# Two transfers into an unread place in HBM, behind the halves of the next wq, at the change of layers of a decode kernel

## The chip, the cores and the metric

The kernel runs on one core of one Trainium2 chip. The metric is device time in microseconds (us): the median of 3 runs is 673.28 us (673.07 to 673.45).

## The reference

One token goes through attention over a cache, then an MLP, and both once more with the same weights and the same cache. All numbers are float32. Cut to what matters:

```
D, H, Sk, Dh, F = 512, 32, 4096, 128, 1376          # x is [1, 1, 512]

def A(x):                                            # attention over the cache
    q = (x @ wq).reshape(1, 1, H, Dh).transpose(0, 2, 1, 3)
    scores = einsum("bhqd,bhkd->bhqk", q, k_cache) * Dh ** -0.5
    o = einsum("bhqk,bhkd->bhqd", softmax(scores), v_cache)
    return o.transpose(0, 2, 1, 3).reshape(1, 1, H * Dh) @ wo

def B(x):                                            # MLP, gelu by its tanh form
    return gelu(x @ w1 + b1) @ w2 + b2

x = x + A(layernorm(x)); x = x + B(layernorm(x))
x = x + A(layernorm(x)); x = x + B(layernorm(x))
```

## The kernel before

The 32 heads are worked in 8 groups of 4. Each group has 8 MB of K and 8 MB of V (64 KB a partition each) and 1 MB each of wq and wo. One array in SBUF, `arena`, holds everything that is loaded, and the code gives each load its columns in it by hand. Every load goes through the helper `load` (line 87): one DMA issue on SyncE's queue (SP), pinned to the order in which the code writes it. So all transfers run through one hardware queue in that order; a load whose place in `arena` is still being read waits on SP, and with it everything behind it.

Each issue also takes the next of eight completion counters in turn (DMAHW0 to DMAHW7 in the rows below). It waits until the transfer that had its counter before, eight issues earlier, has landed.

Layer 0 takes the groups upwards, layer 1 downwards, so group 7 is last in layer 0 and first in layer 1. Its K and V, and part of the V of group 6, stay in SBUF over the change of layers. Between the two stands the MLP of layer 0 (`mlp`, called with `fill`): `hidden` multiplies by w1 in three parts, `gelu` follows, and a loop over 11 blocks c multiplies by w2 (line 413). w2 lies where the first loads of the next layer go. So the loop itself issues these loads, by the table `follow`: behind block 3 the rest of w2 and the tail of the first chunk of K of group 6; behind block 5 the first half of the next wq (512 KB); behind block 7 its second half; behind block 9 the first 512 KB of that chunk of K. The next wq is group 6's, for the second group of layer 1. Behind the MLP come the rest of that chunk (256 KB), a second chunk of K in two pieces of 512 KB, then two of 1 MB, one of 4 MB, and so on.

With the MLP done, layer 1 makes its queries for group 7 (line 199) and multiplies with the K that stayed (line 232). Meanwhile VectorE makes the queries of group 6 from the two halves of wq (lines 213 and 215, one step for each of four blocks of rows).

`idle` (line 437) is a matmul whose result nobody reads. Only loads and one write at the end use the DMA queue.

Of the kernel before, what the change touches and what calls it, by code (L numbers as in the profile page):

```python
# [12 lines left out]
F32 = mybir.dt.float32  # L13
# [4 lines left out]
P = 128  # L18
# [9 lines left out]
U = 512  # L28
# [25 lines left out]
LAST_IDLE = {3: 1, 5: 1, 6: 1}  # L54
WHOLE, HALVES = ((0, 8),), ((0, 4), (4, 8))
VAR_AT = 1
PAIRS = (0, 2, 4, 6), ((4, 6, 0, 2), (2, 0, 4, 6))


@with_exitstack  # L60
def decode_layers(ctx: ExitStack, tc: tile.TileContext, k, v, w, w1, w2, out):
    nc = tc.nc
# [3 lines left out]

    def ctile(name, *shape):
        return const.tile([P, *shape], F32, name=name)

    smalls, places, uses = ctile("smalls", SMALLS), {}, {}  # L70

    def small(name, n=1):

        if name not in places:
            first = sum(n * len(turns) for n, turns in places.values())
            places[name] = n, [first + n * i for i in range(2 if name in ("xs", "x_sum", "rstd", "sc", "nsc") else 1)]
        uses[name] = uses.get(name, -1) + 1
        turns = places[name][1]
        at = turns[uses[name] % len(turns)]
        assert at + n <= SMALLS and n == places[name][0]  # L80
        return smalls[:, at : at + n]
# [3 lines left out]
    def load(at, src):  # L85
        t = arena[:, at : at + src.shape[-1]]
        tc.keep_in_program_order(nc.sync.dma_start(t, src))  # L87
        return t

    def pin(ins):  # L90
        tc.keep_in_program_order(ins)
# [40 lines left out]
    wq_first = chunk(ahead[:, AHEAD:])  # L132

    ident = ctile("ident", P)
    make_identity(nc, ident)
    nc.vector.memset(negmean, -1.0 / D)
# [20 lines left out]
    def of_32(t, n, i=0):  # L157
        return t[:, : 32 * n].rearrange("p (c q) -> p c q", q=32)[:, :, i]
# [22 lines left out]
    def mean_of(xs, s, at, whole=False, xc=None):  # L181
        nm = minus_mean(s, at, whole)
        sq, ss = small("sq", 4), small("ss")
        xc = small("xc", 4) if xc is None else xc
        nc.vector.tensor_scalar(xc, xs[:, :, 0], nm, None, op0=ALU.add)
        nc.vector.scalar_tensor_tensor(sq, xc, 1.0, xc, op0=ALU.mult, op1=ALU.mult, accum_out=ss)
        return nm, ss, xc

    def rstd_of(ss, at, whole=False):
        nv = minus_mean(ss, at, whole)  # L190
        ve, r = small("ve"), small("rstd")
        tc.keep_in_program_order(
            nc.vector.tensor_scalar(ve, nv, -1.0, EPS, op0=ALU.mult, op1=ALU.add))
        nc.gpsimd.tensor_tensor(r, ve, power, op=ALU.pow)
        return r
# [139 lines left out]
    def mlp(xs, s, w1_t, w2_t, xb, rows, fill, follow):  # L335
        hs, rstd = pH[layer], []
        if fill is None:
            nm, ss, _ = mean_of(xs, s, pN[:, 0:1], True)
            nm_s, nmr, cb, late = small("nm_s"), small("negm"), colsum, HIDDEN[0][1]
            nc.vector.tensor_copy(nm_s, nm)  # L340
        else:
            centred = small("xs", 8).rearrange("p (c i) -> p c i", i=2)
            nc.gpsimd.memset(centred[:, :, 1], 1.0)
            _, ss, _ = mean_of(xs, s, pN[:, 0:1], True, centred[:, :, 0])
        nc.gpsimd.tensor_tensor(xb, xs[:, :, 0], b2c, op=ALU.add)
        if fill is not None:
            xs = centred

        def hidden(i):
            at, first = hs[i], W1_AT[i]  # L350
            n = min(32 * HIDDEN[i][1], FJ) - 32 * HIDDEN[i][0]
            for c in range(4):
                for j in range(J):
                    f = first + n * (J * c + j)
                    pin(nc.tensor.matmul(at[32 * j : 32 * j + 2, :n], xs[:, c, :], w1_t[:, f : f + n],
                                         start=(c == 0), stop=(c == 3)))
                if i == 0 and c == VAR_AT:
                    rstd.append(rstd_of(ss, pN[:, 1:2], True))
                if i == 0 and c == VAR_AT and fill is None:
                    nc.gpsimd.tensor_tensor(nmr, nm_s, rstd[0], op=ALU.mult)  # L360
                    nc.gpsimd.tensor_scalar(cb[:, late:], colsum[:, late:], nmr, None, op0=ALU.mult)
                    nc.gpsimd.tensor_tensor(cb[:, late:], cb[:, late:], b1c[:, late:], op=ALU.add)

        def turned(i):
            ht = work.tile([P, 32 * 4], F32, name="pt")
            n = HIDDEN[i][1] - HIDDEN[i][0]
            pin(nc.vector.transpose(ht[:, : 32 * n], hs[i][:, : 32 * n]))  # L367
            return ht

        def gelu(i, ht):  # L370
            b0, b1_ = HIDDEN[i]
            n = b1_ - b0
            h, u, g = (small("gelu_" + k, FB)[:, b0:b1_] for k in "hug")
            if fill is not None:
                pin(nc.vector.scalar_tensor_tensor(u, of_32(ht, n), rstd[0], b1c[:, b0:b1_], op0=ALU.mult, op1=ALU.add))  # L375
                nc.gpsimd.tensor_copy(colsum[:, b0:b1_], of_32(ht, n, 1))
            elif i > 0:
                pin(nc.vector.scalar_tensor_tensor(u, of_32(ht, n), rstd[0], cb[:, b0:b1_], op0=ALU.mult, op1=ALU.add))
            else:
                pin(nc.vector.scalar_tensor_tensor(h, of_32(ht, n, 1), nm_s, of_32(ht, n), op0=ALU.mult, op1=ALU.add))  # L380
                pin(nc.vector.scalar_tensor_tensor(u, h, rstd[0], b1c[:, b0:b1_], op0=ALU.mult, op1=ALU.add))
            nc.scalar.activation(g, u, AF.Gelu_apprx_tanh)  # L382
            if fill is not None and b1_ == FB:
                nc.scalar.activation(small("m"), g[:, :1], AF.Exp, scale=0.0)
            return g

        if fill is not None:
            idle(fill, pS, 2 * P)
        hidden(0)
        if fill is None:  # L390
            hidden(1)
            pin(nc.vector.transpose(rows[:, P : 2 * P], rows[:, :P]))
        ht = turned(0)
        if fill is None:
            hidden(2)
        else:
            idle(fill, pO)
        for i, (b0, b1_) in enumerate(HIDDEN):
            if i == 1 and fill is not None:
                for n in (512, 256):  # L400
                    idle(fill, pS, n)
                hidden(1)
                ht = turned(1)
                idle(fill, pS, 2 * P)
            g = gelu(i, ht)
            if fill is None and b1_ < FB:
                ht = turned(i + 1)
            for c in range(b0, b1_):
                if c == b0 + 2 and i == 1 and fill is not None:
                    hidden(2)  # L410
                    ht = turned(2)
                for j in range(J):
                    pin(nc.tensor.matmul(pM[32 * j : 32 * j + 1, :], g[:, c - b0 : c - b0 + 1],
                                         w2_t[c][:, P * j : P * (j + 1)], start=(c == 0), stop=(c == FB - 1)))
                for at, src in follow.get(c, ()):
                    load(at, src)
            if i == 1 and fill is not None:
                idle(fill, pS, 2 * P)

# [16 lines left out]
    def idle(t, at, n=512):  # L436
        pin(nc.tensor.matmul(at[:C, :n], ident[:, :C], t[:, 0, :n], start=True, stop=True))  # L437

    for layer in range(2):
# [23 lines left out]
        for n, g in enumerate(order):  # L463
            first, final = n == 0, n == G - 1
            pairs = None
            if layer == 0 and n < G - 2:
                pairs = PAIRS[0]
            if layer == 1 and 1 < n < G - 2:
                pairs = PAIRS[1][n % 2]

# [146 lines left out]
        if layer == 0:  # L617
# [6 lines left out]
                9: ((SPARE, first_k[:, : 2 * U]),),  # L624
            }
        mlp(x1, s1, w1_t, w2_t[layer], xb, *((None, last_v) if layer == 0 else (ends, None)), follow)
        if layer == 0:
            idle(last_v, pS, 2 * P)
# [57 lines left out]
```

## Time and profile before

| what | value |
|---|---|
| median of 3 runs | 673.28 us |
| the profiled execution | 673.77 us |
| its span | 672.0 us |
| DMA queue busy, of 16 engines | 99.1% |
| moved | 285 MB, mean 425 GB/s |
| TensorE / VectorE / ScalarE busy | 45% / 61% / 32% |
| share of the chain that ended last: DMA / TensorE / VectorE | 65% / 16% / 15% |

The span runs from the first instruction to the last; the profiled execution's own time is 1.77 us longer. The chain is followed back from the last instruction, at each step to what released it. KB in the rows are 1024 bytes; "us to landing" runs from the issue on SP to the landing of the transfer's last byte.

### The profile page before, as it was taken

To read this page: it belongs to the slowest core of one execution; us is meant where nothing else is said; L and a number is where in the kernel's file an instruction comes from. 1 tells how busy PE (TensorE), PEld (TensorE's weight loads), DVE (VectorE), ACT (ScalarE), POOL (GpSimd) and SP (SyncE) were. 2 spreads that over 40 slices of the span, in tenths; PEclk is the share of its full clock that TensorE was granted. 3 is DMA by queue.
4 is the path that set the end of the run, shared out by engine and by line. 5 is a ranking of instruction groups with operands and counts; after the bars stand their busy time and mean duration, and the time that the engine had idled before them with its cause. 6 is when DMAs were issued, how large, how long until landed. Compare 5 with 4: busy or idle time off the path is not lost.

```text
span 672.0 us, 6011 instructions
## 1 busy us (share of the span) xinstructions
PE 301.1 (45%) x2236; PEld 79.4 (12%) x2236; DVE 406.7 (61%) x510; ACT 215.4 (32%) x697; POOL 5.2 (1%) x26
## 2 busy tenths in 40 slices
PE   1501603416016053166698985604316026065597
PEld 1100100101001010011124311101001001011124
DVE  3059679497795876971422313289597794982513
ACT  0047064190560823801011200073290650910010
POOL 1000000000000000000000000000000000000000
PEclk9965855856758557586699998755757758566799
DMA  9999999999999999999999999999999999999997
GB/s 384 429 437 437 438 433 437 410 458 433 437 437 402 466 418 430 421 437 422 429 413 398 391 434 449 426 433 437 421 434 425 433 430 415 456 429 418 429 416 301
DMA packets 11548, 285.36 MB, mean 425 GB/s; under 512 B 1280, under 2 KB 1408, under 8 KB 3840
## 3 DMA queue, kind: packets, MB, share of 16 engines
q1 hardware_dynamic: 11520, 284.99, 99.1%
q8 instruction: 17, 0.28, 0.2%
q14 instruction: 11, 0.09, 0.0%
HBM read 284.92 MB, written 0.07 MB: 424 GB/s over the span
## 4 chain that ended last, share of the span: by engine, by line
DMA 65%; PE 16%; DVE 15%; issue 1%; another core or an unknown queue 1%; SPq 0%; ACT 0%; DVEq 0%; ACTq 0%
DMA arena<-in_v 38%; DMA arena<-in_k 19%; DMA arena<-in_w 8%; PE pS L232 7%; DVE arena L274 7%; PE pO L262 5%; DVE arena L279 3%; DVE arena L311 2%; DVE arena L287 1%; PE pO L283 1%; DVE arena L215 1%; PE pB L323 1%; SPq L87 0%; DVE arena L309 0%
## 5 line engine op out<-in xcount | busy, mean ns | idle before, releaser
L269 ACT ACTIVATE arena<-arena,pt 128x128 f32<-128x128 f32 x640 | 188.0, 387 | 49.1 <-DMA arena<-in_v 45.3
L232 PE MATMUL pS<-arena,smalls 128*8 128x512 f32 x1024 | 147.3, 728 | 78.6 <-DMA arena<-in_k 74.5
L279 DVE TENSOR_TENSOR arena<-arena 128x4096 f32<-128x4096 f32 x30 | 132.6, 4420 | 0.3
L217 PE MATMUL pS<-arena,smalls 128*128 128x512 f32 x20 | 20.7, 1140 | 203.4 <-DVE arena L215 203.4
L274 DVE TENSOR_TENSOR arena<-arena,pt 128x2048 f32<-128x2048 f32 x40 | 89.0, 2286 | 37.3 <-DMA arena<-in_v 34.6
L244 ACT ACTIVATE arena<-pS,smalls 128x512 f32<-128x512 f32 x16 | 12.4, 777 | 292.8 <-DVE smalls L243 292.8
L287 DVE STREAM_TRANSPOSE arena<-pO 128x512 f32<-128x512 f32 x16 | 11.5, 717 | 98.3 <-PE pO L262 60.9
L232 PEld LDWEIGHTS pS<-arena,smalls 128*8 128x8 f32 x1024 | 29.8, 102 | 199.1 <-issue 178.6
L262 PE MATMUL pO<-arena,pt 128*4 128x512 f32 x368 | 46.8, 653 | 10.8 <-DMA arena<-in_v 10.0
L236 DVE TENSOR_REDUCE smalls<-pS 128x1 f32<-128x512 f32 x16 | 11.0, 687 | 62.7 <-PE pS L232 62.7
L215 DVE SCALAR_TENSOR_TENSOR arena<-arena,smalls 128x512 f32<-128x512 f32 x45 | 33.8, 752 | 1.6
L311 DVE SCALAR_TENSOR_TENSOR arena<-arena,smalls 128x512 f32<-128x512 f32 x39 | 29.3, 752 | 1.4
L217 PEld LDWEIGHTS pS<-arena,smalls 128*128 128x128 f32 x20 | 5.0, 312 | 206.1 <-DVE arena L215 206.1
L315 PE MATMUL pB<-arena,smalls 128*1 128x512 f32 x26 | 14.1, 625 | 29.8 <-DVE arena L311 29.8
L246 PE MATMUL pO<-ident,arena 128*128 128x128 f32 x64 | 12.2, 320 | 25.6 <-ACT arena L244 25.2
L572 DVE TENSOR_TENSOR arena<-arena 128x2048 f32<-128x2048 f32 x10 | 22.9, 2292 | 0.3
L262 PEld LDWEIGHTS pO<-arena,pt 128*4 128x4 f32 x368 | 10.0, 92 | 44.4 <-issue 37.5
L382 ACT ACTIVATE smalls<-smalls 128x4 f32<-128x4 f32 (+1 forms) x6 | 1.2, 205 | 42.6 <-DVE smalls L375 24.7
L250 DVE STREAM_TRANSPOSE smalls<-smalls 128x32 f32<-128x32 f32 x16 | 3.4, 212 | 17.5 <-ACT arena L244 17.5
L437 PE MATMUL pS<-arena,ident 128*8 128x512 f32 (+1 forms) x30 | 12.9, 522 | 0.5 <-DVE pt L367 0.5
L244 ACT ACT_TABLE_LOAD x1 | 1.3, 1283 | 35.9 <-DVE smalls L243 35.9
L246 PEld LDWEIGHTS pO<-ident,arena 128*128 128x128 f32 x64 | 7.6, 155 | 39.5 <-ACT arena L244 34.1
(115 smaller groups left out, 186.2 us busy)
## 6 DMA issues: line engine op xcount, KB each, us to landing
arena<-in_w SPq DMA_DIRECT2D x13, 2048.0 KB, 12.5
arena<-in_k SPq DMA_DIRECT2D x5, 4096.0 KB, 22.3
arena<-in_v SPq DMA_DIRECT2D x2, 4096.0 KB, 32.8
arena<-in_w SPq DMA_DIRECT2D x6, 1024.0 KB, 30.7
arena<-in_k SPq DMA_DIRECT2D x1, 6144.0 KB, 21.0
arena<-in_v SPq DMA_DIRECT2D x2, 2048.0 KB, 37.3
arena<-in_w SPq DMA_DIRECT2D x7, 512.0 KB, 11.4
arena<-in_v SPq DMA_DIRECT2D x3, 1024.0 KB, 47.3
```

The costliest lines, as they stand in the source:

```text
L215: pin(nc.vector.scalar_tensor_tensor(t, wt[:, c, :], xc[:, c : c + 1], t, op0=ALU.mult, op1=ALU.add))
L217: pin(nc.tensor.matmul(at, one.to_broadcast([P, P]), t, start=True, stop=True))
L232: pin(nc.tensor.matmul(pS[32 * j : 32 * j + C, :], z[:, j, C - 1 - c : 2 * C - 1 - c], kt[:, j, :], start=(c == 0), stop=(c == C - 1)))
L246: nc.tensor.transpose(pT[:, b].rearrange("p j r -> p (j r)"), p[:, P * b : P * (b + 1)], ident)
L262: nc.tensor.matmul(pO[32 * j : 32 * j + 4, :], pt[:, j, c, :], by_head(vt)[:, j], start=(i == 0), stop=(i == of - 1))
L269: nc.scalar.activation(own, own, AF.Copy, scale=pt[:, j, c, b : b + 1])
L274: nc.vector.tensor_tensor(own, own, weight, op=ALU.mult)
L279: pin(nc.vector.tensor_tensor(a, a, b, op=ALU.add))
L287: nc.vector.transpose(ot[:, :512], pO)
L311: pin(nc.vector.scalar_tensor_tensor(t, wt[:, d, :], on[:, d : d + 1], t, op0=ALU.mult, op1=ALU.add))
L315: pin(nc.tensor.matmul(pB[0:1, :], one, t, start=n == 0, stop=n == G - 2))
L572: pin(nc.vector.tensor_tensor(total, total, other, op=ALU.add))
```

## The change

Two tiles of 128 rows of 2 KB are made in HBM. Behind the issue of each half of the next wq, one transfer copies 2 KB a partition (256 KB) of w1 from HBM into one of them. Nothing reads these tiles. It is issued on the same queue, SP's, and pinned to its place.

```
+IDLE_TRANSFERS = (5, 7)
...
+    spare_dram = ctx.enter_context(tc.tile_pool(name="spare_dram", bufs=1, space=bass.MemoryType.DRAM))
+    unread = [spare_dram.tile([P, U], F32, name=f"unread{i}") for i in range(2)]
+
+    def idle_transfer(i):
+        pin(nc.sync.dma_start(unread[i], w1[:, U * i : U * (i + 1)]))
...
                 for at, src in follow.get(c, ()):
                     load(at, src)
+                if fill is not None and c in IDLE_TRANSFERS:
+                    idle_transfer(IDLE_TRANSFERS.index(c))
```

On SP's queue, from the tail of K (128x512) through the pieces of K behind the change, stood before (L87 is `load`; the sizes are partitions x elements of 4 bytes; the names in brackets are what an issue waits for):

```order
L87 DMA arena<-in_k 128x512 [waits DMAHW5_49,PE_49]
L87 DMA arena<-in_w 128x1024 [waits DMAHW0_49,PE_49]
L87 DMA arena<-in_w 128x1024 [waits DMAHW7_49,DMAHW2_49,PE_49]
L87 DMA arena<-in_k 128x1024 [waits DMAHW3_49,PE_49]
L87 DMA arena<-in_k 128x512 [waits DMAHW4_49,DMAHW1_49,PE_49]
L87 DMA arena<-in_k 128x1024 [waits PE_49] x2
L87 DMA arena<-in_k 128x2048 [waits PE_49]
L87 DMA arena<-in_k 128x2048 [waits DMAHW5_49,PE_49]
L87 DMA arena<-in_k 128x8192 [waits DMAHW6_49,PE_49]
```

In the same place stands now (`load` is L94, the idle transfer L75):

```order
L94 DMA arena<-in_k 128x512 [waits DMAHW5_49,PE_49]
L94 DMA arena<-in_w 128x1024 [waits DMAHW0_49,PE_49]
L75 DMA unread_66<-in_w 128x512 [waits DMAHW7_49]
L94 DMA arena<-in_w 128x1024 [waits DMAHW2_49,PE_49]
L75 DMA unread_67<-in_w 128x512 [waits DMAHW1_49]
L94 DMA arena<-in_k 128x1024 [waits DMAHW3_49,PE_49]
L94 DMA arena<-in_k 128x512 [waits DMAHW4_49,PE_49]
L94 DMA arena<-in_k 128x1024 [waits PE_49]
L94 DMA arena<-in_k 128x1024 [waits DMAHW5_49,PE_49]
L94 DMA arena<-in_k 128x2048 [waits DMAHW6_49,PE_49]
L94 DMA arena<-in_k 128x2048 [waits DMAHW7_49,PE_49]
L94 DMA arena<-in_k 128x8192 [waits DMAHW0_49,PE_49]
```

Two issues came in, and the counters behind them moved on by one and by two: the last 128x2048 piece now waits for the counter that the first idle transfer uses (DMAHW7), and the one ahead of it for that of the first half of wq (DMAHW6).

On VectorE, in the queries of group 6 that use the next wq, stood before (L213 is the first block of rows, L215 the other three):

```order
L461 TENSOR_SCALAR smalls<-smalls 128x1
L213 TENSOR_SCALAR arena<-arena,smalls 128x512 [waits DMAHW6_49]
L215 SCALAR_TENSOR_TENSOR arena<-arena,smalls 128x512 [waits DVE_49]
L215 SCALAR_TENSOR_TENSOR arena<-arena,smalls 128x512 [waits DMAHW7_49,DVE_49]
L215 SCALAR_TENSOR_TENSOR arena<-arena,smalls 128x512 [waits DVE_49]
```

and now:

```order
L470 TENSOR_SCALAR smalls<-smalls 128x1
L220 TENSOR_SCALAR arena<-arena,smalls 128x512 [waits DMAHW6_49]
L222 SCALAR_TENSOR_TENSOR arena<-arena,smalls 128x512 [waits DVE_49]
L222 SCALAR_TENSOR_TENSOR arena<-arena,smalls 128x512 [waits DMAHW0_49,DVE_49]
L222 SCALAR_TENSOR_TENSOR arena<-arena,smalls 128x512 [waits DVE_49]
```

Nothing moved here; the second half of wq is waited for at the same step as before (the second of the three), under another counter's name.

## Rows read from the trace of the kernel before

**Rows 1.** The page: the DMA queue (packets, MB, share), and the chain by engine.

```profile
q1 hardware_dynamic: 11520, 284.99, 99.1%
DMA 65%; PE 16%; DVE 15%; issue 1%; another core or an unknown queue 1%; SPq 0%; ACT 0%; DVEq 0%; ACTq 0%
```

**Rows 2.** The chain in order of time: start us, us, what.

```profile
371.29 7.05 PE pS L232 x64
...
414.33 23.56 DMA arena<-in_v
...
656.72 11.43 DMA arena<-in_w
...
668.28 0.99 PE pO L413 x24
```

**Rows 3.** By stretches: us, busy time (count) of each engine, PEclk, DMA share, GB/s.

```profile
342.00:366.00 24.00, 20.75 (x296) 8.19 (x296) 3.81 (x16) 0.41 (x2) 1.13 (x4) 1.00 1.01 413
366.00:376.00 10.00, 8.76 (x137) 3.46 (x134) 5.05 (x19) 1.69 (x3) 0.84 (x3) 1.00 0.93 319
378.00:402.00 24.00, 21.95 (x158) 5.66 (x153) 3.93 (x15) 3.61 (x8) 0.00 (x0) 1.00 1.03 441
```

**Rows 4.** The timeline of SP's issues: start us, us of the issue itself.

```profile
360.74 0.38 SPq L87 DMA_DIRECT2D arena<-in_w  x1
361.22 0.38 SPq L87 DMA_DIRECT2D arena<-in_k  x1
364.78 0.33 SPq L87 DMA_DIRECT2D arena<-in_w  x1
367.01 0.33 SPq L87 DMA_DIRECT2D arena<-in_w  x1
368.37 0.33 SPq L87 DMA_DIRECT2D arena<-in_k  x1
373.25 0.33 SPq L87 DMA_DIRECT2D arena<-in_k  x1
409.13 0.33 SPq L87 DMA_DIRECT2D arena<-in_k  x1
```

**Rows 5.** DMA issues: KB, us to landing; those of rows 4, then 368.3 to 374.

```profile
arena<-in_w SPq DMA_DIRECT2D x1, 256.0 KB, 7.5
arena<-in_k SPq DMA_DIRECT2D x1, 256.0 KB, 7.7
arena<-in_w SPq DMA_DIRECT2D x1, 512.0 KB, 5.4
arena<-in_w SPq DMA_DIRECT2D x1, 512.0 KB, 4.4
arena<-in_k SPq DMA_DIRECT2D x1, 512.0 KB, 5.4
arena<-in_k SPq DMA_DIRECT2D x1, 1024.0 KB, 10.1
arena<-in_k SPq DMA_DIRECT2D x1, 2048.0 KB, 12.0
arena<-in_k SPq DMA_DIRECT2D x2, 1024.0 KB, 9.3
arena<-in_k SPq DMA_DIRECT2D x3, 512.0 KB, 6.2
arena<-in_k SPq DMA_DIRECT2D x1, 256.0 KB, 5.6
```

**Rows 6.** VectorE's timeline where it uses the next wq.

```profile
372.16 0.48 DVE L213 TENSOR_SCALAR arena<-arena,smalls 128x512 f32<-128x512 f32 x1
372.67 2.33 DVE L215 SCALAR_TENSOR_TENSOR arena<-arena,smalls 128x512 f32<-128x512 f32 x3
```

**Rows 7.** DMA issues into an empty queue: the kernel's first load, its last write.

```profile
arena<-in_w SPq DMA_DIRECT2D x1, 1056.0 KB, 4.8
out<-arena SPq DMA_DIRECT2D x1, 64.0 KB, 1.5
```

## The prediction

> **What bounds the kernel now.** I read the page's queue section and its chain first, then the chain in order of time, then the DMA share by stretches, and last the issues one by one. One hardware queue moves 285 MB and keeps 16 engines 99.1% busy, and 65% of the chain that ended last is DMA [rows 1]. The chain ends in a transfer that lands at 668.1 us, then 1.0 us of matmuls [rows 2]. So the kernel ends when its slowest DMA engine has moved all bytes, and the rest counts only where it lets the queue run dry.
>
> It runs dry once, at the change of layers. The queue moves 413 GB/s from 342 to 366 us and 441 GB/s from 378 to 402 us, but 319 GB/s from 366 to 376 us [rows 3]. That is 10 us x (413 - 319) / 413 = 2.3 us of lost transfer time. The reader is to see that TensorE runs at its full granted clock (1.00) in all three stretches, so its clock is no part of this.
>
> The issues say where the time is lost. A transfer's last byte lands at its issue time plus its time to landing [rows 4, 5]: the 256 KB of the k tail (issued 361.22) at 368.92, the first half of the next wq (364.78) at 370.18, the second half (367.01) at 371.41, the first piece of K (368.37) at 373.77, the last of the small pieces of K (373.25) at 383.35. At 413 GB/s a piece of 512 KB takes 1.27 us. The first half of wq comes 1.26 us behind the k tail and the second 1.23 us behind the first: up to 371.41 the last engine loses nothing. The first piece of K comes 2.36 us later, so 1.09 us are lost there. From then to 383.35 are 9.58 us for 256 + 2 x 512 + 2 x 1024 KB (3328 KB, 3.41 MB), which take 8.25 us at 413 GB/s: another 1.33 us lost. Together 2.4 us, as the stretch of 10 us gave it.
>
> Behind 378 us the queue stays ahead: a K transfer issued at 409.13 lands only at 421.1 [rows 4, 5], and the load of V that the chain names is issued at 414.33 into that backlog [rows 2]. From 371 to 414 us the chain runs on TensorE and VectorE [rows 2] with data landed long before, so a small shift of the queue does not reach it. Whatever moves the landing at 383.35 moves the end by as much, unless it is lost and won again inside the change.
>
> **The change part by part.** It adds two DMA issues on SP, one behind each half of the next wq, each moving 256 KB from HBM to HBM. It removes and reorders nothing; a later load merely has one or two more transfers between it and the one that last used its completion counter.
>
> *SP's time.* An issue takes 0.33 to 0.38 us [rows 4]. The first stands between 365.1 and 367.01, the second between 367.34 and 368.37: both in gaps in which SP waits for matmuls, 1.9 and 1.0 us long. Cost nothing. If a gap were too short, the first piece of K would be issued up to 0.4 us later.
>
> *Completion counters.* There are eight in turn, so each issue waits for the transfer eight places earlier. The 1 MB piece issued at 373.25 now waits for the first idle transfer instead of an older load, and the one before it for the first half of wq, which landed at 370.18. The idle one should land near 370.9, over 2 us before it is needed. Nothing; it would cost only if that transfer took over 3 us.
>
> *The later landing of wq.* The second half lands one idle transfer later, 371.41 + 0.68 = 372.1. VectorE starts on the first half at 372.16 and needs the second for the second of its three 0.78 us steps from 372.67, at about 373.4 [rows 6]. Hidden, with 1.3 us to spare.
>
> *The bytes themselves.* This is the term that counts. The trace has no transfer from HBM to HBM. The nearest row is a load of the same 256 KB in 2 KB rows with a full queue: issued 360.74, landed 368.24, and the next such 256 KB at 368.92, so 0.68 us [rows 4, 5]. Two cost 1.36 us where the queue is full. The lower bound is zero, where they run in time that is lost anyway. The upper bound is 1.5 us each: the 64 KB that the kernel writes to HBM land 1.5 us after issue with nothing ahead [rows 7], all of it start and finish. A load into a cold queue shows as much of its own: 4.8 us for 1056 KB that take 2.6 us at 413 GB/s, 2.2 us of start and finish [rows 7], so a write to HBM does not look slower to finish than a load. I take 0.68 us.
>
> The Trainium skill speaks against that value: its page "DMA: Bandwidth & Descriptors", section "Latency and other measured facts", gives 214 GB/s per direction as the full rate of copies between HBM tensors. By it an idle transfer would take an estimated 262,144 B / 214 GB/s = 1.22 us, 2.4 us for both; no row here shows one, and the sum does not use it.
>
> *The sum for the slowest engine.* First half of wq 370.18, idle 370.86, second half 372.13, idle 372.81, first K piece 372.81 + 1.27 = 374.08 against 373.77 before: +0.31 us. Of 1.36 us added, 1.05 fill the 1.09 us that this engine lost there. Behind it the second loss, 1.33 us, is still to come. If it comes from late issues, the times of which TensorE sets, the +0.31 vanishes in it wholly or in part; so the landing at 383.35 moves by 0 to +0.3. On the engines that ran ahead the idle transfers lie wholly in time lost. I take +0.2 us. Against the profiled execution (span 672.0, 673.77 in all) that gives 674.0; that execution was 0.49 us above the median of the runs, so against the median, 673.28, it gives **673.5 us**.
>
> **The rivals.**
>
> *The queue stays warm.* A good part of the loss may not be late issue but the start of a queue run dry: the first piece of K needs 5.4 us from issue to landing though only 371.41 + 1.27 was in its way, and 2.2 us of start and finish show at the kernel's start [rows 5, 7]. If an idle transfer in front lets the engines fetch the next one's work beneath it, the second loss goes too: +0.31 - 1.33 = -1.0 us, **672.3**. Against it: the later pieces of K are issued in step with TensorE's work on the new layer, at times no idle transfer changes. Even wholly right it gives at most 2.4 - 1.36 = 1.0 us.
>
> *A packet from HBM to HBM costs more than a load (the slower side).* It reads and writes the same memory, and the engine may hold it twice as long: 1.36 us instead of 0.68. Then the second half of wq lands at 372.8, the first K piece at 371.41 + 2 x 1.36 + 1.27 = 375.4, +1.67 us, of which the second loss takes none if it is a start-up loss: **674.95**, slower. If it takes all of its 1.33, +0.3. The point is where two transfers exceed 1.05 us of cover by the 1.35 us that can be told: 1.2 us each. At the upper bound of 1.5 us it is +1.95, **675.2**. For it: the same HBM serves both sides. Against: the queue is bound by its engines at 413 to 441 GB/s whatever the load, and the write at the end shows nothing long.
>
> The rate of 214 GB/s in "DMA: Bandwidth & Descriptors" (the Trainium skill, section "Latency and other measured facts") stands behind this rival: its 1.22 us lie just at that point.
>
> *No cover.* If the first K piece came late for want of its own data path and not because of its issue time, idle work ahead of it only adds: +1.36, **674.6**, at the edge of what can be told.
>
> *It doesn't do what it says.* If a transfer from HBM to HBM were spread over few of the 16 engines, one engine would carry 256 KB alone: 16 x 0.64 = 10 us each. Nothing in the loads, all cut by 128 rows, suggests it.
>
> **How the numbers follow.** A difference of 0.2% (1.35 us) is about what a measurement of this kernel can tell from no change. Chances: forecast (-0.3 to +0.6 us) 0.54; warm queue (-1.2 to -0.3) 0.2; costlier packets 0.16, half of it over +1.35; no cover 0.07, half of it over; few engines 0.03. Faster by over 0.2% would need all the lost time back and the idle bytes free, which only a mis-read loss allows: 0.06, out of the warm queue. Slower: 0.08 + 0.04 + 0.03 = 0.15. The same: 0.79. The range goes from the warm queue's 672.3 to the costlier packet's upper bound, 675.2; the likeliest case's own is 673.0 to 673.9.
>
> **What would show it.** Right: two rows of 256 KB into the unread place that take about 0.7 us of the queue each; the stretch 366 to 376 us up from 319 GB/s by nearly the 52 GB/s that 0.52 MB bring; the second half of wq landing near 372.1, the first piece of K near 374, the last small piece at 383.0 to 383.7, and 414.33 for the issue of V unchanged. Warm queue: the last small piece near 382.3. Costlier packets: the first piece of K past 375. Wrong altogether: the matmuls or VectorE's steps at 371 to 374 us waiting for wq, or issues of K held behind the idle transfers' completion.

## The result, and the profile after

The changed kernel takes 674.23 us (median of 22 runs, 673.96 to 674.49), the kernel before 673.09 us (22 runs beside it, 672.67 to 674.82). The ratio is 1.0013, 95% interval 1.0007 to 1.0019: +0.9 us, between +0.5 and +1.3. It is estimated from all runs, so it is not the quotient of the two medians, which differ by 1.14 us. The forecast was 673.5 us, +0.2, too little to be told from no change. The measured time lies in the range and under the 0.2% bound, but clear of zero. In a second measurement (the fifth experiment) the same kernel gave 1.0007 (0.9998 to 1.0015), +0.5 us. A second difference was not forecast: the runs of before spread over 2.2 us (standard deviation 0.54), those after over 0.5 us (0.14). Beside experiments 5 to 8 one run of before fell in a slow state (712.36 us); it is left out below.

The page of after, the lines of [rows 1], and the bytes to and from HBM:

```profile
q1 hardware_dynamic: 11808, 285.51, 99.2%
HBM read 285.44 MB, written 0.59 MB: 425 GB/s over the span
DMA 63%; PE 17%; DVE 16%; another core or an unknown queue 2%; issue 1%; SPq 0%; ACT 0%; DVEq 0%; ACTq 0%
```

There are 288 packets more (2 x 128, and 16 x 2 that write the counters), and 0.52 MB more are read and written. The change does what it says. By stretches, as in [rows 3]:

```profile
342.00:366.00 24.00, 20.57 (x298) 8.00 (x298) 4.16 (x18) 0.41 (x2) 1.27 (x6) 1.00 1.00 411
366.00:376.00 10.00, 8.95 (x134) 3.57 (x138) 4.71 (x18) 1.69 (x3) 0.70 (x2) 1.00 1.04 385
378.00:402.00 24.00, 21.70 (x158) 5.57 (x152) 4.09 (x16) 3.51 (x7) 0.00 (x0) 1.00 1.05 448
```

The stretch of the change moves 385 GB/s where it moved 319. But 52 of the 66 GB/s more are idle bytes, and 319 was a low draw: two further profiles of the kernel before (experiments 1 and 9) moved 353 and 350 there:

```profile
366.00:376.00 10.00, 8.62 (x130) 3.47 (x134) 5.02 (x19) 1.69 (x3) 0.83 (x3) 1.00 0.99 353
366.00:376.00 10.00, 8.71 (x134) 3.55 (x138) 4.92 (x19) 1.69 (x3) 0.73 (x2) 1.00 0.98 350
```

SP's issues as in [rows 4], and with them those of the idle transfers (L75):

```profile
361.89 0.38 SPq L94 DMA_DIRECT2D arena<-in_k  x1
364.43 0.33 SPq L94 DMA_DIRECT2D arena<-in_w  x1
364.81 0.60 SPq L75 DMA_DIRECT2D unread<-in_w  x1
366.67 0.34 SPq L94 DMA_DIRECT2D arena<-in_w  x1
367.07 0.50 SPq L75 DMA_DIRECT2D unread<-in_w  x1
368.04 1.00 SPq L94 DMA_DIRECT2D arena<-in_k  x1
372.94 0.33 SPq L94 DMA_DIRECT2D arena<-in_k  x1
```

and the landings of the same seven, in the same order, as in [rows 5]:

```profile
arena<-in_k SPq DMA_DIRECT2D x1, 256.0 KB, 6.7
arena<-in_w SPq DMA_DIRECT2D x1, 512.0 KB, 5.4
unread<-in_w SPq DMA_DIRECT2D x1, 256.0 KB, 5.7
arena<-in_w SPq DMA_DIRECT2D x1, 512.0 KB, 5.0
unread<-in_w SPq DMA_DIRECT2D x1, 256.0 KB, 5.3
arena<-in_k SPq DMA_DIRECT2D x1, 512.0 KB, 5.8
arena<-in_k SPq DMA_DIRECT2D x1, 1024.0 KB, 10.1
```

Added up: K tail 368.59, first half of wq 369.83, idle 370.51, second half 371.67, idle 372.37, first K piece 373.84, last 1 MB piece 383.04. The idle transfers cost 0.68 and 0.70 us, the price taken (a time to landing is given to 0.1 us, so each of these differences is good to about 0.1). From the tail to the last piece are 14.45 us; the useful bytes take 12.06 (4.98 MB at 413 GB/s), so 2.39 us go elsewhere, 1.36 of them into idle bytes and 1.03 into waiting. In the profile of before the same stretch lost 2.37 us [rows 4, 5]. By these two profiles the change would cost nothing. VectorE does not notice, as in [rows 6]:

```profile
371.85 0.48 DVE L220 TENSOR_SCALAR arena<-arena,smalls 128x512 f32<-128x512 f32 x1
372.36 2.33 DVE L222 SCALAR_TENSOR_TENSOR arena<-arena,smalls 128x512 f32<-128x512 f32 x3
```

The load of V that the chain names is issued 0.2 us earlier than in [rows 2], and the chain ends 0.2 us later:

```profile
414.13 26.00 DMA arena<-in_v
...
656.95 11.40 DMA arena<-in_w
668.35 0.14 issue
668.48 1.00 PE pO L420 x24
```

Spans are 672.4 against 672.0 us, yet the medians differ by 1.1. So the question for the experiments: where does the rest come from, and how far does one profile of before stand for its runs? Each was timed beside the kernel before on the same chip. The loss given with each is that of the last engine: the time from the K tail's landing to the last 1 MB piece's, less 12.06 us. (The expectations quote some losses read more finely; they differ from those here by up to 0.05 us.) A spread is the standard deviation of a kernel's runs.

### The profile page after: what moved, and what is told of

It is laid out like the page before. It is cut to its first block, busy times and chain, and to the rows that moved or that the text cites. A ratio compares the mean times of both kernels' runs of the same rounds, so it can differ in the third digit from the quotient of the medians.

```text
span 672.4 us, 6015 instructions
## 1 busy us (share of the span) xinstructions
PE 302.4 (45%) x2236; PEld 79.7 (12%) x2236; DVE 406.8 (61%) x510; ACT 215.4 (32%) x697; POOL 5.2 (1%) x26
## 4 chain that ended last, share of the span: by engine, by line
DMA 63%; PE 17%; DVE 16%; another core or an unknown queue 2%; issue 1%; SPq 0%; ACT 0%; DVEq 0%; ACTq 0%
DMA arena<-in_v 31%; DMA arena<-in_k 24%; DMA arena<-in_w 8%; PE pS L239 8%; DVE arena L281 7%; PE pO L269 5%; DVE arena L286 3%; DVE arena L318 2%; DVE arena L294 1%; PE pO L290 1%; DVE arena L222 1%; PE pB L330 1%; DVE arena L316 1%; PE pO L233 0%
## 5 line engine op out<-in xcount | busy, mean ns | idle before, releaser
L239 PE MATMUL pS<-arena,smalls 128*8 128x512 f32 x1024 | 145.3, 720 | 79.2 <-DMA arena<-in_k 75.0
L322 PE MATMUL pB<-arena,smalls 128*1 128x512 f32 x26 | 15.8, 693 | 29.6 <-DVE arena L318 29.6
```

The source lines that it names most:

```text
L239: pin(nc.tensor.matmul(pS[32 * j : 32 * j + C, :], z[:, j, C - 1 - c : 2 * C - 1 - c], kt[:, j, :], start=(c == 0), stop=(c == C - 1)))
L322: pin(nc.tensor.matmul(pB[0:1, :], one, t, start=n == 0, stop=n == G - 2))
```

## The experiments

**1. The kernel before, again.** No edit.

> The kernel before, unchanged, profiled and timed once more: how far one profile of it stands for its median. The changed kernel measured +0.9 us (ratio 1.0013), while the two profiles differ by 0.4 us of span. Theory A (the idle bytes cost the last engine most of their 1.36 us, and the first profile of before showed more lost time at the change than a usual run has): the same time as before within 0.2 us, a span near 671.4 instead of 672.0, and less than the 2.4 us lost between the k tail's landing and that of the last 1 MB piece of K, near 1.6 us. Theory B (the cost is not at the change but a fixed one of two more issues or of another program): again 2.4 us lost there.

Median 674.08 us against 673.73; ratio 1.0008 (0.9998 to 1.0017). So the medians of kernels that are the same can stand 0.35 us apart, with 11 runs of one. Its issues of the K tail and the last 1 MB piece, and their landings:

```profile
361.94 0.39 SPq L87 DMA_DIRECT2D arena<-in_k  x1
373.25 0.33 SPq L87 DMA_DIRECT2D arena<-in_k  x1
```

```profile
arena<-in_k SPq DMA_DIRECT2D x1, 256.0 KB, 6.9
arena<-in_k SPq DMA_DIRECT2D x1, 1024.0 KB, 9.4
```

368.84 to 382.65: 1.75 us lost, not 2.37, as theory A had it (1.6). The span, 672.0, was as long as in the first profile of before, though the last piece landed 0.70 us earlier: it lost elsewhere what it gained here.

**2. Almost no bytes.**

```
-        pin(nc.sync.dma_start(unread[i], w1[:, U * i : U * (i + 1)]))
+        pin(nc.sync.dma_start(unread[i][:, :16], w1[:, U * i : U * i + 16]))
```

> The two idle transfers move 64 B a partition instead of 2 KB: same issues, places and completions, 1/32 of the bytes. Theory A (bytes): at most 0.1 to 0.2 us over the kernel before, ratio 1.0000 to 1.0003. Theory B (fixed cost of the issues, of their completions or of a write to HBM): the same +0.9 us as the changed kernel, ratio 1.0013. Theory C (an idle transfer keeps the queue warm whatever its size): faster than before by 0.2 to 1 us.

674.35 us, ratio 1.0012 (1.0003 to 1.0021); its median stands 0.27 us above that of experiment 1, an unchanged kernel, with runs that spread by 0.9. By its time this neither shows nor excludes a fixed cost. Its loss is 2.54 us (368.87 to 383.47): 64 B a partition do not keep the queue from running dry, which ends theory C. Its quickest run, 673.08, is as quick as before's (672.97), while no run of the changed kernel has come under 673.96.

**3. Twice the bytes.**

```
-    unread = [spare_dram.tile([P, U], ...
+    unread = [spare_dram.tile([P, 2 * U], ...
-        pin(nc.sync.dma_start(unread[i], w1[:, U * i : U * (i + 1)]))
+        pin(nc.sync.dma_start(unread[i], w1[:, 2 * U * i : 2 * U * (i + 1)]))
```

> The two idle transfers move 4 KB a partition, twice the bytes of the change. At 1.27 us each they add 2.54 us to each engine's queue. Theory A (bytes, the cover already used up by the first 1.36 us): +0.9 + 1.2 = +2.1 us over before, ratio 1.0031. Theory B (fixed): +0.9 us as the changed kernel, ratio 1.0013. If much of the lost time can still be filled, something between, near +1.4.

675.71 us (6 runs), ratio 1.0032 (1.0020 to 1.0044): +2.2 us as theory A had it; theory B, a cost that is all fixed (1.0013), is out. A fixed part beside the price of the bytes is not: theory A's sum takes the +0.9 of the first measurement as given. Its issues of the K tail and the last piece, and their landings:

```profile
361.07 0.38 SPq L94 DMA_DIRECT2D arena<-in_k  x1
373.13 0.33 SPq L94 DMA_DIRECT2D arena<-in_k  x1
```

```profile
arena<-in_k SPq DMA_DIRECT2D x1, 256.0 KB, 7.7
arena<-in_k SPq DMA_DIRECT2D x1, 1024.0 KB, 11.2
```

368.77 to 384.33: 3.50 us, of which 2.54 are idle bytes and 0.96 waiting. With twice the bytes the waiting stays at 1.0 us. What idle bytes can replace was replaced by the first ones; in these profiles the rest was not filled from these places.

**4. Two transfers where the queue is full.** The call moves from `mlp` to the fourth group of layer 0.

```
-                if fill is not None and c in IDLE_TRANSFERS:
-                    idle_transfer(IDLE_TRANSFERS.index(c))
...
+                if layer == 0 and n == 3:
+                    idle_transfer(0)
+                    idle_transfer(1)
```

> Both idle transfers of 2 KB a partition stand in layer 0, behind the weights of the fourth group, where the queue is never dry, instead of at the change of layers: the full price of the bytes with no cover. Theory A: +1.36 us over before, ratio 1.0020, so the change of layers covers 1.36 - 0.9 = 0.4 to 0.5 us. If a transfer from HBM to HBM cost twice a load of its size: +2.7 us, ratio 1.0040. Theory B (fixed cost of the issues): +0.9 us.

674.84 us, ratio 1.0015 (1.0006 to 1.0024): +1.0 us. The issues of the weights and the two idle transfers, and their landings:

```profile
170.01 0.33 SPq L94 DMA_DIRECT2D arena<-in_w  x1
170.39 0.59 SPq L75 DMA_DIRECT2D unread<-in_w  x1
171.04 0.58 SPq L75 DMA_DIRECT2D unread<-in_w  x1
```

```profile
arena<-in_w SPq DMA_DIRECT2D x1, 2048.0 KB, 11.6
unread<-in_w SPq DMA_DIRECT2D x1, 256.0 KB, 11.9
unread<-in_w SPq DMA_DIRECT2D x1, 256.0 KB, 11.9
```

181.61, 182.29, 182.94: 0.68 and 0.65 us each. A transfer from HBM to HBM costs what a load of its size costs, and the rival of the dearer packet falls. The +1.36 expected lies in the interval, as does theory B's +0.9. The interval (+0.4 to +1.6) also holds what the change itself cost: by these times no cover at all is shown for the change of layers.

**5. The changed kernel, again.** No edit.

> The changed kernel, unchanged, timed and profiled once more beside the kernel before. Its first measurement gave ratio 1.0013 (+0.9 us), but the profile shows its last engine losing 2.34 us at the change (1.36 us of idle bytes among them) against 2.41, 1.70 and 2.55 us in three profiles without such bytes (the kernel before, the same again, and the one with 64 B a partition). Theory A (the idle bytes fill lost time but for 0.1 to 0.7 us): +0.1 to +0.7 us, ratio 1.0002 to 1.0010, 2.0 to 2.6 us lost again. Theory B (a cost of 0.9 us or more that the change of layers doesn't show): +0.9 to +1.1 us, ratio 1.0013 to 1.0016. Both: a spread of its runs far below that of the kernel before (standard deviation 0.14 against 0.5 to 0.7 us).

674.42 us against 673.50; ratio 1.0007 (0.9998 to 1.0015), spread 0.12 us. The K tail (issued 361.11, 7.7 us to landing) lands at 368.81, the last piece (373.17, 10.1 us) at 383.27: 2.40 us lost, 1.04 of it waiting, as in its first profile (2.39, 1.03). The interval holds theory A (1.0002 to 1.0010) and B's lower end.

**6 and 7. One transfer alone.** `IDLE_TRANSFERS = (5,)`, then `(7,)`.

> Only the idle transfer behind the first half of the next wq is left. Theory A1 (the first 0.7 us of idle bytes are covered, what comes above is not, since the kernel with 4 KB a partition cost 1.2 us more than the changed one for 1.2 us more of bytes): 0 to +0.2 us against before, ratio 1.0000 to 1.0003. Theory A2 (a byte costs the same whichever it is): half of the changed kernel's cost, +0.3 to +0.5 us. If this place has no cover of its own, since the last engine loses nothing ahead of the second half of wq: +0.7 us.

> Only the idle transfer behind the second half of the next wq is left, right ahead of the first piece of K, where the engines ran dry. Theory A1: 0 to +0.2 us, ratio 1.0000 to 1.0003, and no more than with the first one alone. Theory A2: +0.3 to +0.5 us. The warm queue: faster than before by 0.2 to 0.7 us, since the engines reach the first piece of K without a break.

673.83 and 673.77 us beside 673.50; ratios 1.0001 (0.9992 to 1.0010) and 0.9999 (0.9990 to 1.0007), spreads 0.15 and 0.13 us. The two places do not differ, though one has lost time right behind it and the other has none. Losses 1.88 and 2.00 us, 1.20 and 1.32 of it waiting. No gain from a warm queue shows, though the second's interval reaches down to -0.7 us. A1 fits; A2 (+0.3 to +0.5) is not excluded.

**8. Two transfers farther back.** `IDLE_TRANSFERS = (9, 10)`.

> Both idle transfers of 2 KB a partition stand behind the first piece of K and the last product of the MLP instead (blocks 9 and 10), in front of the 256, 512 and 512 KB pieces of K, where the second part of the lost time lies. If the loss there is late issue: covered as well as in the changed kernel, +0.1 to +0.7 us. If it is the start of a dry queue, the fill works best here: 0 to -0.7 us. If the cover lies at the first piece of K alone: the full price, +1.3 us, ratio 1.0019.

674.45 us, ratio 1.0010 (1.0001 to 1.0019): about the changed kernel's cost; the full price (1.0019) is the interval's upper end. Its profile lost 3.06 us (368.57 to 383.69), 1.70 of it waiting: no better cover, and no gain from bridging the later pieces.

**9. The kernel before, a third time.** No edit.

> The kernel before a third time, for one more profile of the change of layers and for the spread of its runs. So far the kernels without real idle bytes (before, the same again, 64 B a partition) lose 2.41, 1.70 and 2.55 us there and their runs spread by 0.5 to 0.9 us of standard deviation; those with 2 KB or more at the change spread by 0.12 to 0.15. Theory S1 (the spread is the dry queue's: how late each engine starts again differs from run to run): a loss between 1.6 and 2.6 us that goes with this run's time, spread 0.5 to 0.9 us. Theory S2 (the spread comes from elsewhere and the idle bytes only shift what meets what): the same spread, but a loss that does not go with the time.

673.51 us, ratio 0.9999 (0.9987 to 1.0011), spread 0.92 us. Issues and landings of the K tail and the last piece:

```profile
362.13 0.38 SPq L87 DMA_DIRECT2D arena<-in_k  x1
373.15 0.33 SPq L87 DMA_DIRECT2D arena<-in_k  x1
```

```profile
arena<-in_k SPq DMA_DIRECT2D x1, 256.0 KB, 6.7
arena<-in_k SPq DMA_DIRECT2D x1, 1024.0 KB, 9.3
```

368.83 to 382.45: 1.56 us lost. Three profiles of before give 2.37, 1.75 and 1.56 us in executions of 673.77, 673.82 and 673.55 us: the loss differs from run to run, and the time does not simply follow it. With three profiles this speaks for S2 and does not prove it.

**10. One transfer where the queue is full.** As 4, with `idle_transfer(0)` alone.

> One idle transfer of 2 KB a partition, in layer 0 where the queue is never dry, none at the change of layers. Full price: 0.65 us if a transfer from HBM to HBM costs a load of its size (two of them there cost 1.1 us by median, 1.3 us of queue time by profile). +0.5 to +0.7 us over before, ratio 1.0008 to 1.0010. Theory S1: its runs spread as those of the kernel before do (0.5 to 0.9 us), since the change is as dry as before. Theory S2: they may spread little (0.15 to 0.35).

674.28 us against 673.73, ratio 1.0004 (0.9995 to 1.0013); the expected 1.0008 to 1.0010 lies inside. Spread 0.43 us, between what S1 and S2 said. In 4 and in this kernel no idle bytes stand at the change, so their profiles are two more draws of its loss. The K tail and the last piece, of 4 and then of 10:

```profile
362.22 0.90 SPq L94 DMA_DIRECT2D arena<-in_k  x1
374.27 0.33 SPq L94 DMA_DIRECT2D arena<-in_k  x1
362.60 0.38 SPq L94 DMA_DIRECT2D arena<-in_k  x1
373.75 0.33 SPq L94 DMA_DIRECT2D arena<-in_k  x1
```

```profile
arena<-in_k SPq DMA_DIRECT2D x1, 256.0 KB, 7.7
arena<-in_k SPq DMA_DIRECT2D x1, 1024.0 KB, 9.0
arena<-in_k SPq DMA_DIRECT2D x1, 256.0 KB, 6.8
arena<-in_k SPq DMA_DIRECT2D x1, 1024.0 KB, 9.9
```

369.92 to 383.27 in 4, 369.40 to 383.65 in 10: 1.29 and 2.19 us lost. So the loss without idle bytes lies between 1.29 and 2.37 us in five profiles, 1.83 on average.

**11. A quarter of the bytes.** The slice is `[:, :P]`, 512 B a partition.

> Both idle transfers at the change, with 512 B a partition instead of 2 KB: 0.22 us of each engine's queue each, 0.43 in all. By the bytes (the first 0.7 us covered): 0 to +0.2 us against before, ratio 1.0000 to 1.0003. Theory S1: too few bytes to bridge the dry stretch, a spread between that of 64 B (0.88) and of 2 KB (0.14), near 0.5 us. Theory S2: no forecast.

674.46 us against 673.73, ratio 1.0004 (0.9994 to 1.0015). Its spread is 0.79 us, above the 0.5 that S1 had; 1.58 us lost (368.97 to 382.61).

All runs together, each kernel against the runs of before beside it:

| kernel | idle bytes, us of the queue | quickest run over before's | median over before's | standard deviation of its runs |
|---|---|---|---|---|
| before (1) / (9) | 0 | +0.30 / -0.13 | +0.35 / -0.22 | 0.90 / 0.92 |
| 64 B (2) | below 0.1 | +0.11 | +0.62 | 0.88 |
| 512 B (11) | 0.3 (128 KB at 413 GB/s; 0.43 in its expectation) | +0.41 | +0.73 | 0.79 |
| first (6) / second (7) alone | 0.68 | +0.64 / +0.65 | +0.33 / +0.27 | 0.15 / 0.13 |
| one, full queue (10) | 0.68 | +0.81 | +0.55 | 0.43 |
| the change / again (5) | 1.36 | +1.29 / +1.18 | +1.14 / +0.92 | 0.14 / 0.12 |
| two, farther back (8) | 1.36 | +1.34 | +0.95 | 0.26 |
| two, full queue (4) | 1.36 | +1.52 | +1.11 | 0.35 |
| 4 KB (3) | 2.54 | +2.61 | +1.98 | 0.14 |

The third column follows the second: in its best runs a kernel pays nearly the full price of its idle bytes wherever they stand. A quickest run is one run, and beside the experiments there are more than twice as many runs of before to be quick in: the unchanged kernel itself stands at +0.30 and -0.13. The +0.11 and +0.41 with 64 B and 512 B leave little room for a large fixed cost. The medians are smaller than the third column from 0.68 us on; the runs of before have a long upper end (to 675.69 us) that most of these kernels have less of (the highest of 4 and 10 are 675.57 and 675.32).

The profiles tell the same by another path, from the K tail's landing to the end of the span. Without idle bytes at the change this took 303.1 (before), 303.2 (1), 302.9 (9), 302.7 (4) and 303.1 us (10); with the change 303.8 both times; with one transfer 303.2 both times (6, 7); with two farther back 303.9 (8); with 4 KB 305.0 (3); with 512 B 302.9 (11). Over the mean of the five, 303.0, the change costs 0.8 us, one transfer 0.2 and 4 KB 2.0. One profile doesn't fit: 64 B took 304.4 (2), in an execution that was 0.7 us above its kernel's median.

## Why the prediction was right, and where it was off

*What bounds the kernel*: right. Idle bytes where the queue is full cost their queue time by the landings of 4, and at the change nearly as much (3: +2.2 us for 2.54).

*SP, counters, landing of wq*: right in that none costs anything. The issues of the idle transfers took 0.50 to 0.60 us instead of the 0.33 to 0.38 reckoned with, still inside SP's waits. Behind them the issue of the first piece of K held SP for 1.00 us instead of 0.33, which the prediction did not foresee; the last 1 MB piece was issued no later for it (372.94, before 373.25). The second half of wq landed 0.69 us before VectorE's 372.36, the next steps unmoved.

*The price of the bytes*: right, 0.68 us taken, 0.65 to 0.70 measured (4 and the profile after). No run here shows the 214 GB/s that the Trainium skill gives for copies between HBM tensors ("DMA: Bandwidth & Descriptors", "Latency and other measured facts"): 262,144 B in 0.65 to 0.70 us are 375 to 403 GB/s, and the measurement decides. (For the dearer packet the prediction has +1.67 us; by its own landings, 375.4 against 373.77, it is 1.63, which changes nothing.)

*The sum*: mis-sized in one term, the cover. The prediction let 1.05 of the 1.36 us fill time that the last engine lost anyway, on the strength of one profile that lost 2.37 us, and took the second loss to swallow some of the rest. Four more profiles lost 1.29 to 2.19 us. With the mean of the five, 1.83 us, the changed kernel's 2.39 and 2.40 cost 0.6 us, so by the loss the cover is about 0.8 us; by the time from the K tail to the end it is about 0.55, and by the quickest runs 0.1 to 0.2. These are estimates from few executions, and the size of the cover stays open; none of them reaches 1.05.

*From the landing to the end*: "Whatever moves the landing at 383.35 moves the end by as much" is not borne out. With the change the last piece landed 0.31 us earlier than in the first profile of before, and the span ended 0.4 us later. From that landing to the end of the span took 288.65 us in the first profile of before and 288.85 in 10, the two with the largest losses, but 289.25 to 289.36 in 1, 9, 4 and both of the change. So what was lost at the change was in part won again by the end; by what, no run shows. That is 0.7 us of the rest that the first two profiles left open; besides, the profiled execution of before, 673.77 us, was itself 0.68 us above the median of its runs, 673.09.

*The signs*: what the prediction said would show it right came out, all but the time itself: two rows of about 0.7 us, the stretch up from 319 to 385 GB/s, the first piece of K near 374 (373.84), the last piece within 383.0 to 383.7 (383.04 and 383.27). The cost of +0.9 us instead of +0.2 does not show in any of them. That the time lies in the range is partly the range's width: 672.3 to 675.2 holds every rival but few engines, and +0.9 is nearer to the +1.36 of "no cover", which had a chance of 0.07, than to the +0.2 of the forecast. How much of the first measurement's +0.9 is luck of the runs of before there, the runs do not say.

*Which part can be covered*: the prediction split the loss into 1.09 and 1.33 us and could not say of the second whether it was late issue or a queue gone cold. With idle bytes at these places about 1.0 us of waiting stays, at 1.36 us of them as at 2.54 (3, 5). Idle bytes take up the part above that, which was 0.3 us in one profile without them and 1.4 in another. That the remaining 1.0 us is late issue fits, but no run moved the issues, so it is not shown.

*The rivals*: the warm queue fell with the result (1.0 us faster forecast, +0.5 to +1.3 measured), the dearer packet fell (4), few engines fell (4). "No cover" comes nearest for the best runs, by the table. The waiting is shorter with idle bytes, by 0.8 us (1.83 to 1.03), but the bytes cost more than that. A small fixed cost of two more issues, beside that of the bytes, was not tested with enough runs to be ruled out.

Open is why kernels with 2 KB a partition or more behind the halves of wq have a spread of at most 0.15 us (8: 0.26) while before's is 0.5 to 0.9. That the dry stretch alone makes the spread (S1) is not borne out: in three profiles before's loss does not go with its time (9), and idle bytes in layer 0, which leave the change to run dry, narrow the spread too (4: 0.35, 10: 0.43).

No kernel with idle bytes beats the kernel before.

## What to carry to other kernels

Where a kernel ends when its DMA queue has moved all bytes, price idle transfers like loads: here a gap that lost 1.3 to 2.4 us covered at most some 0.8 us of 1.36. A gap read from one profile is one draw: profile the unchanged kernel again before taking its length as cover, above all when the whole question is about one microsecond. Follow the loss to the end of the span, too: what one landing in the middle lost may be won again behind it. And compare spreads and quickest runs beside medians; here the change cost nearly its bytes in the best runs, and its slowest runs were quicker than the slowest of before.

## What the runs showed of the hardware

A copy from HBM to HBM in rows of 2 KB ran at the rate of a load from HBM to SBUF, 0.65 to 0.70 us for 256 KB. Its issue held SP longer: 0.50 to 0.60 us against the usual 0.33 to 0.38 of a load and 0.35 of the kernel's last write, which goes to HBM too (at 669.61 in the profile before); single issues of loads took as long or longer (1.00 us at 368.04 in the profile after). And one kernel's time to come through the same stretch of transfers, on the last of 16 engines, varied by 0.8 us over three profiles.
